# Row bounds as 16 rows of the query tile, gate logits inside the value projections, and one form for every VectorE key tile, in a fused attention and feed-forward kernel

## The chip, the cores and the metric

The kernel runs on one core of one Trainium2 chip. The metric is device time in microseconds (us) of one execution. A core has TensorE (matrix multiply, PE), VectorE (DVE), ScalarE (ACT), GpSimd (POOL) and SyncE (SP, which here issues nearly all DMAs). [...]

## The reference

```
x: (1, 2048, 512) bf16; 32 heads of 16; feed-forward width 1792
g = sigmoid((x * gate_w).sum(-1, keepdims=True))
q, k, v = split(x @ wqkv)                       # per head (2048, 16)
p = softmax(q @ k.T * 16 ** -0.5)
a = concat_heads(p @ v) @ wo
b = (silu(x @ w_gate) * (x @ w_up)) @ w_down
out = g * a + (1 - g) * b
```

## The kernel before

Queries are split into four blocks of 512 (`qb`), heads into eight groups of four (`g`). A unit is one block and one group, 32 units in all, and each has 16 key tiles of 128 keys: 512 key tiles. For one key tile the scores of four heads are four matrices of 128 keys by 512 queries; their exponentials are multiplied with the values by `pv`, four matmuls side by side (one per head) in the 32-column strips of the array, into one accumulating PSUM bank `o_ps`. Column 0 of each head's values is one, so row 0 of each strip sums the softmax denominators.

Two engines compute exponentials. ScalarE takes a key tile as two pairs of heads: `emit_pair` (line 741) writes scores to a two-bank tile `s_t` (two of them, in turn), one ACTIVATE of 128x1024 writes `e_t`. VectorE takes a whole key tile: `emit_d` (line 808) sends each head's scores to a one-bank tile `d_t`, and a scale, an addition and a conversion to uint16 make the bits of a rough bf16 exponential in `y` (tile names c_t, kaug, wd_t, by the buffer it was given). That is then refined in one of two ways, by `groups[n]`:

- 2: two mask instructions (`bits`, line 858) and one product (`product`, line 867) give two bf16 tiles, so two groups of four value matmuls;
- 4: three additions of constants (`copy`, line 850) give four tiles, so four groups of value matmuls.

`v_take` (line 1471) asks `quad` (line 1479): it gives 4 when the planned idle time of TensorE, summed in `spare`, is over `SPARE`, and else 2.

The softmax subtracts a bound instead of the row's maximum. A row of `kaug` (the keys, 32 rows per head) is constant, and the query tile's row 0 of each head holds minus the sum over 16 dimensions of |q| times the largest |k| of that dimension (`kb`, from `k_bound`, line 467). Rows 1 to 16 hold q and k. For the groups 1 to 7, `q_pieces` (line 532) projects the queries, copies them to `qst`, sends them by DMA to the query tiles `q1` and `qx` (`get_q`), and takes absolute values into `aq`; `bound_pieces` (line 600) multiplies `aq` with `kneg` on TensorE, copies the result to `bq` and sends it by DMA to row 0. Group 0 has its own path, which uses the same row.

The values of heads 4 to 31 are projected per key tile by `v_pieces` (line 507); `gate_pieces` (line 624) makes the gate's logits with 64 one-column matmuls, and `gate_end` (line 640) their exponential.

The order on each engine is not left to a scheduler. While the program is built, a planner keeps a time for each engine (`plan.pe`, `plan.dve`, `plan.act`), with a cost for each instruction (0.6 us for an eviction, `MUL_US` for a product), and emits instructions one by one; `ordered` ties each to the one before it on its engine. ScalarE's pairs come first. Gaps of TensorE are filled with value matmuls and with pieces of chains (projections, feed-forward, output), which `Pacer` picks by release and deadline in slots (one slot per key tile). `fill_dve` (line 887) gives VectorE the next thing that is ready. `v_unit` (line 1454) lets VectorE take another key tile from the end of a unit when it would be done in time; so the number of key tiles on VectorE, and with it that of ScalarE's exponentials, comes out of the planner. Everything but `s_t` and `o_ps` shares three PSUM banks (`m_tile`, line 358): `d_t`, projections, the feed-forward's `gu` and `dps`, the output's `ops`.

Of the kernel before, what the change touches and what calls it, by code (L numbers as in the profile page):

```python
# [79 lines left out]
def kernel(  # L80
# [46 lines left out]
    EXP_B = {4: 128.0 * (127.0 - math.log2(5.372947814979324)), 2: 128.0 * (127.0 - math.log2(1.5015118813815151))}  # L127
    MUL_US = 1.2
    TINY = 1e-37
    AHEAD = 1  # L130
    SPARE = 0.5

# [75 lines left out]
    def late_loads():  # L208
        queue.dma_start(out=gw_col[:], in_=gate_w.rearrange("(dc p) -> p dc", p=P))
        queue.dma_start(out=wo_t[:], in_=A_wo.rearrange("(b p) d -> p b d", p=P))  # L210
        for i in range(2):
            for j in range(4):
                h = H - 8 + 4 * i + j
                queue.dma_start(out=wo_l[32 * j + 1:32 * j + 1 + DH, i, :], in_=A_wo[h * DH:(h + 1) * DH, :])
# [41 lines left out]
    for g in (1, 2):  # L256
# [11 lines left out]

    pidx = const.tile([P, 1], F32, name="pidx")
    nc.gpsimd.iota(pidx[:], pattern=[[0, 1]], base=0, channel_multiplier=1,  # L270
                   allow_small_or_imprecise_dtypes=True)
    bsel = const.tile([P, 8], BF16, name="bsel")
    lo_t = const.tile([P, 8], F32, name="lo_t")
    for h in range(8):
        c = 2 * (h % 4) + h // 4
        nc.gpsimd.memset(lo_t[:, c:c + 1], float(DH * h))
    far_t = const.tile([P, 8], F32, name="far_t")
    nc.gpsimd.memset(wo_l[:], 0.0)
# [10 lines left out]
    kb = const.tile([P, NB], F32, name="kb")  # L289
    kneg = const.tile([P, NB, 8], BF16, name="kneg")  # L290
    gval = const.tile([P, KT], F32, name="gval")
# [156 lines left out]
    def k_pieces(b, tb):  # L448

        def end(t, p):  # L450
            vec.tensor_copy(out=kst[b][:, t * QBW:(t + 1) * QBW], in_=p[:, :])
            m_free(p, plan.dve)
            if t == QB - 1:
                for hh in range(8):
                    g, j = 2 * b + hh // 4, hh % 4
                    if g > 0:
                        queue.dma_start(out=kaug[32 * j + 1:32 * j + 1 + DH, g, :],
                                          in_=kst[b][DH * hh:DH * (hh + 1), :])

        def lhs(dc):  # L460
            if dc == 0 and tb == 0:
                kst[b] = (on_t[1], bblk)[b == 1][:, :, :].rearrange("p b q -> p (b q)")
            return wqk[:, dc, D + P * b:D + P * (b + 1)]
        return columns(DC, "kp", lhs, lambda dc: xT[:, dc, tb * QBW:(tb + 1) * QBW],
                       lambda p: later(0.6, lambda: end(tb, p)))

    def k_bound(b):
        vec.tensor_reduce(out=kb[:, b:b + 1], in_=kst[b][:, :], axis=AX.X, op=ALU.max, apply_absolute_value=True)
        vec.tensor_scalar(out=kneg[:, b, :], in0=bsel[:, :], scalar1=kb[:, b:b + 1],
                          scalar2=None, op0=ALU.mult)  # L470

# [35 lines left out]
    def v_pieces(tt):  # L507

        def end(p):
            dst = vaug[:, tt, 4 * VC:G * 4 * VC].rearrange("p (h c) -> p h c", c=VC)[:, :, 1:1 + DH]  # L510
            vec.tensor_copy(out=dst, in_=p[:, 64:D].rearrange("p (h c) -> p h c", c=DH))
            m_free(p, plan.dve)
        return columns(DC, "vp", lambda dc: xT[:, dc, tt * P:(tt + 1) * P], lambda dc: wv[:, dc, 64:D],
                       lambda p: later(0.54, lambda: end(p)), c0=64)

# [6 lines left out]
    for g in range(5, G):  # L522
# [3 lines left out]
          for qb in range(QB)]  # L526
    aqs = {}

# [3 lines left out]
    def q_pieces(qb, b):  # L532
        def landed(p):
            me = plan.chain
            later(0.6, lambda: end(p, me), key=("q", b))

        def end(p, me):
            qst = work.tile([P, QBW], BF16, tag="qst", name="qst")
            vec.tensor_copy(out=qst[:, :], in_=p[:, :])
            m_free(p, plan.dve)  # L540
            for hh in range(8):
                gg, j = hh // 4, hh % 4
                if (b, gg) != (0, 0):
                    queue.dma_start(out=get_q(qb, 2 * b + gg)[32 * j + 1:32 * j + 1 + DH, j % 2, :],
                                      in_=qst[DH * hh:DH * (hh + 1), :])

            def mag():
                aq = work.tile([P, QBW], BF16, tag="aq", name="aq", bufs=4)
                vec.tensor_scalar(out=aq[:, :].bitcast(U16), in0=qst[:, :].bitcast(U16),
                                  scalar1=0x7FFF, scalar2=None, op0=ALU.bitwise_and)  # L550
                aqs[(qb, b)] = aq
            plan.chain = me
            later(0.21, mag, plan.dve, ("q", b))
# [31 lines left out]
    def variants(p, to, q, more=()):  # L585
# [11 lines left out]
        for cost, f in more:  # L597
            later(cost, f, key=key)

    def bound_pieces(qb, b):  # L600

        st = {}

        def f():
            st["p"] = m_tile("bp")
            mm(st["p"][0:8, :], lhsT=kneg[:, b, :], rhs=aqs[(qb, b)][:, :], start=True, stop=True,
               tile_position=(0, 0))
            spend("C", 1)
            later(0.6, end)

        def end():
            bq = work.tile([8, QBW], BF16, tag="bq", name="bq")
            vec.tensor_copy(out=bq[:, :], in_=st["p"][0:8, :])
            m_free(st["p"], plan.dve)
            for j in range(4):
                if b == 0:
                    queue.dma_start(out=q1[32 * j:32 * j + 1, j % 2, :], in_=bq[2 * j + 1:2 * j + 2, :])
                else:
                    t = qx[(qb * (NB - 1) + b - 1) % 2]
                    queue.dma_start(out=t[32 * j:32 * j + 1, j % 2, :, :], in_=bq[2 * j:2 * j + 2, :])  # L620
        return [(1, f, True)]


    def gate_pieces(t0):
        def f():
            gp = m_tile("glog")
            for t in (t0, t0 + 1):
                for dc in range(DC):
                    mm(gp[:, t:t + 1], lhsT=xT[:, dc, t * P:(t + 1) * P],
                       rhs=gw_col[:, dc:dc + 1], start=(dc == 0), stop=(dc == DC - 1))  # L630
            spend("F", 2)

            def end():
                vec.tensor_scalar(out=ge[:, t0:t0 + 2], in0=gp[:, t0:t0 + 2], scalar1=-40.0, scalar2=40.0,
                                  op0=ALU.max, op1=ALU.min)
                m_free(gp, plan.dve)
            later(0.15, end)
        return [(0.7, f, True, "F", None)]

# [80 lines left out]
    groups = {}  # L720
    spare = [0.0]
    pv_turn = [True]
# [426 lines left out]
    for g in (3, 4):  # L1149
        ones_rows(vec, g)  # L1150

    vec.tensor_scalar(out=lo_t[:], in0=lo_t[:], scalar1=pidx[:, 0:1], scalar2=None, op0=ALU.subtract)
    vec.tensor_scalar(out=far_t[:], in0=lo_t[:], scalar1=-float(DH) + 0.5, scalar2=-1.0,
                            op0=ALU.is_gt, op1=ALU.mult)
    vec.scalar_tensor_tensor(out=bsel[:, :], in0=lo_t[:], scalar=0.5, in1=far_t[:],
                                   op0=ALU.is_lt, op1=ALU.mult)
    plan.act = plan.pe
# [54 lines left out]
    q_of[0] = again  # L1212
    v_rest = [pace.add(v_pieces(tt), 2, int(12 + 3 * tt)) for tt in range(KT)]

# [14 lines left out]
    for qb in range(QB):  # L1229
        for b in range(NB):  # L1230
# [16 lines left out]
            else:  # L1247
                rel = UNIT.index((qb, 2 * b - 2)) * KT + 1 if (qb, b) != (0, 2) else UNIT.index((0, 2)) * KT + 1
            q = pace.add(q_pieces(qb, b), rel, d - 25)
            bc = pace.add(bound_pieces(qb, b), rel, d - 22, [q] + after, 2)  # L1250
            need.setdefault(d - 12, []).append(bc)
            for g in {max(2 * b, 1), 2 * b + 1}:
                q_of[UNIT.index((qb, g))] = bc
    gates = [pace.add(gate_pieces(2 * i), 36 + 7 * i, 44 + 7 * i) for i in range(KT // 2)]
    gates = [pace.add([(0.2, gate_end, False)], 40, 106, gates)]
    turned = pace.add([(1, turn_odds, True, "F", None)], 40, 130, gates, 2)
# [120 lines left out]
    def begin(n):  # L1377
        plan.slot = n
        for c in need.get(n, []):
            force(c)  # L1380
        if n == 28:
            late_loads()
# [88 lines left out]
    def v_take():  # L1471
        un = v_unit()
        hi[un] -= 1
        n = un * KT + hi[un]
        groups[n] = 2 if quad() else 4
        forward()
        return n

    def quad():
        if spare[0] > SPARE:  # L1480
            spare[0] = 0.0
            return False
        return True

# [10 lines left out]
    while au < UNITS:  # L1495
# [10 lines left out]
        if room > 0.02:  # L1506
# [17 lines left out]
            if room > 0.4 and closed in o_of and 0 < pvs[closed] and pv_left(closed) > 1 and (closed or pvs[0] != KT // 2) and sum(  # L1524
# [5 lines left out]
                spend("C", 1)  # L1530
                spare[0] += 0.22
                continue
            if room > 0.15:
                plan.pe += 0.1
                spare[0] += 0.1
                continue
# [98 lines left out]
```

## Time and profile before

| | |
|---|---|
| three runs, median (range) | 780.24 us (780.03 to 782.4) |
| the profiled execution | 780.74 us; span in the profile 778.8 us |
| granted TensorE clock | 0.999 |
| busy of the span: ScalarE, TensorE, VectorE | 764.5, 740.7, 725.5 us |
| first and last exponential of ScalarE start at | 13.16 us, 769.7 us |
| DMA | 32.63 MB in 88138 packets |

A line of the costliest groups reads: source line, engine, operation, output<-input by tile names, partitions x elements and type, count | busy us, mean ns of one | idle time just before them and what ended it. All instructions that the planner orders carry the line of the helper (163, 166, 175), so tile names tell them apart. Instructions of one engine overlap a little: the time from start to start is shorter than one's duration. A wait is read as: who waited <- for whom: total us, times, the longest.

### The profile page before, as it was taken

The page shows a single profiled execution, that of the slowest core. Times are in us where ns is not written, and L with a number is a line of the kernel's source. Part 1 is how long each engine was busy: PE and PEld are TensorE (multiplying, and loading weights), DVE is VectorE, ACT ScalarE, POOL GpSimd, SP SyncE. Part 2 cuts the span into 40 slices and gives each one's busy share as a digit, 9 for nine tenths or more (in the row PEclk, how much of TensorE's full clock was granted, in tenths as well). Part 3 has the DMA queues.
Part 4 walks back from the last instruction along what each step waited for, and adds up shares of the span by engine and source line. Part 5 has one row for each costly group of instructions (what it writes and reads, how often), then busy time and mean ns, then how long its engine had stood idle before and what let it go on. Part 6 is the DMA issues. An engine that isn't in the chain of part 4 may idle for free.

```text
span 778.8 us, 21608 instructions
## 1 busy us (share of the span) xinstructions
PE 740.7 (95%) x8877; PEld 223.6 (29%) x8877; DVE 725.5 (93%) x1162; ACT 764.5 (98%) x863; POOL 11.0 (1%) x34
## 2 busy tenths in 40 slices
PE   8999999999999999999999999989999989999997
PEld 3322333322222222232222222222222322222222
DVE  7799999899889999999999999999999999999994
ACT  5999999999999999999999999999999999999996
POOL 5000000000000000000000000000000000000000
PEclk9999999999999999999999999999999999999999
DMA  8002103134110112220100131211001222100001
GB/s 189 2 5 49 29 20 79 50 99 94 43 32 8 27 37 62 51 53 20 32 15 19 31 94 26 66 28 34 13 20 27 60 66 45 46 12 12 15 29 35
DMA packets 88138, 32.63 MB, mean 42 GB/s; under 512 B 74304, under 2 KB 87592, under 8 KB 88040
## 3 DMA queue, kind: packets, MB, share of 16 engines
q1 hardware_dynamic: 86312, 30.93, 16.5%
q8 instruction: 69, 1.13, 0.6%
q10 hardware_dynamic: 1728, 0.33, 0.2%
q14 instruction: 29, 0.24, 0.1%
HBM read 21.55 MB, written 2.35 MB: 31 GB/s over the span
## 4 chain that ended last, share of the span: by engine, by line
ACT 56%; PE 24%; issue 12%; DVE 7%; ACTq 0%; DVEq 0%
ACT e_t L166 53%; PE s_t L163 9%; PE o_ps L163 6%; PE gu L163 5%; DVE c_t L175 4%; ACT th L166 3%; PE qp L163 1%; PE dps L163 1%; DVE mt L175 1%; PE warm L163 1%; PE vp L163 1%; PE kp L163 1%; DVE gs L175 0%; PE ops L163 0%; DVE kaug L175 0%
## 5 line engine op out<-in xcount | busy, mean ns | idle before, releaser
L166 ACT ACTIVATE e_t<-s_t 128x1024 bf16<-128x1024 f32 x794 | 743.7, 1147 | 0.9 <-PE s_t L163 0.8
L175 DVE TENSOR_SCALAR c_t<-d_t 128x512 uint16<-128x512 f32 x404 | 267.8, 683 | 17.7 <-PE d_t L163 17.0
L163 PE MATMUL s_t<-qx,kaug 32*128 32x512 bf16 (+1 forms) x1252 | 244.3, 382 | 21.7 <-ACT e_t L166 19.6
L163 PEld LDWEIGHTS <-kaug 32*128 32x128 bf16 (+1 forms) x2048 | 97.9, 91 | 339.4 <-issue 334.6
L163 PE MATMUL o_ps<-e_t,vaug 128*32 128x512 bf16 x1588 | 154.9, 386 | 0.0
L175 DVE TENSOR_SCALAR c_t<-c_t 128x2048 uint16<-128x2048 uint16 x193 | 129.9, 685 | 1.1
L163 PE MATMUL d_t<-qx,kaug 32*128 32x512 bf16 x380 | 128.5, 384 | 0.0
L163 PE MATMUL o_ps<-c_t,vaug 128*32 128x512 bf16 x1028 | 97.8, 385 | 0.6 <-DVE osb L175 0.6
L163 PEld LDWEIGHTS <-vaug 128*32 128x32 bf16 x2800 | 59.5, 94 | 100.3 <-issue 94.2
L163 PE MATMUL gu<-xT,wg 128*32 128x512 bf16 x896 | 73.0, 384 | 0.0
L175 DVE TENSOR_TENSOR c_t<-c_t 128x2048 bf16<-128x2048 bf16 x59 | 71.7, 1215 | 0.0
L163 PE MATMUL gu<-xT,wu 128*32 128x512 bf16 x896 | 68.3, 382 | 0.1
L163 PE MATMUL ops<-wd_t,mt 128*32 128x512 bf16 x672 | 57.1, 382 | 0.0
L163 PE MATMUL s_t<-q,kaug 32*128 32x512 bf16 (+1 forms) x204 | 39.8, 382 | 6.0 <-ACT e_t L166 5.1
L175 DVE SCALAR_TENSOR_TENSOR gs<-th,gu 128x512 bf16<-128x512 bf16 x56 | 38.2, 682 | 3.4 <-ACT th L166 3.0
L175 DVE SCALAR_TENSOR_TENSOR mt<-gs,gu 128x512 bf16<-128x512 bf16 x56 | 38.2, 682 | 3.2 <-PE gu L163 1.5
L166 ACT ACTIVATE th<-gu 128x512 bf16<-128x512 f32 x56 | 40.9, 731 | 0.0
L175 DVE TENSOR_SCALAR kaug<-d_t 128x512 uint16<-128x512 f32 x52 | 34.8, 682 | 1.5 <-PE d_t L163 1.2
L163 PEld LDWEIGHTS <-mt 128*32 128x32 bf16 (+1 forms) x1037 | 24.1, 95 | 27.5 <-issue 21.6
L163 PEld LDWEIGHTS <-wu 128*32 128x32 bf16 x896 | 19.5, 95 | 24.1 <-issue 15.2
L163 PEld LDWEIGHTS <-wg 128*32 128x32 bf16 x896 | 17.4, 94 | 24.3 <-issue 21.8
L175 DVE TENSOR_SCALAR kaug<-c_t 128x2048 uint16<-128x2048 uint16 x35 | 24.0, 686 | 0.3
(149 smaller groups left out, 449.0 us busy)
## 6 DMA issues: line engine op xcount, KB each, us to landing
wg<-in_B_w_gate_dram SPq DMA_DIRECT2D x56, 128.0 KB
wu<-in_B_w_up_dram SPq DMA_DIRECT2D x56, 128.0 KB
on<-osb SPq DMA_DIRECT2D x120, 16.0 KB
rb<-rr SPq DMA_DIRECT2D x15, 128.0 KB
wd_t<-in_B_w_down_dram SPq DMA_DIRECT2D x7, 256.0 KB
qx<-qst SPq DMA_DIRECT2D x96, 16.0 KB
out_dram<-o_t SPq DMA_DIRECT2D x12, 128.0 KB
kaug<-on SPq DMA_DIRECT2D x20, 64.0 KB
```

The source lines that it names most:

```text
L163: return ordered(nc.tensor.matmul(*args, **kw))
L166: ordered(nc.scalar.activation(*args, **kw))
L175: return lambda *a, **kw: ordered(f(*a, **kw))
```

## The change

For groups 1 to 7, q and k now lie in rows 0 to 15 of a head's 32, and rows 16 to 31 hold the bound's 16 terms unsummed: the queries' signs are set to minus, and the result is multiplied by `kb` (a second VectorE instruction), and goes by eight (or four) more DMAs of 16 rows to the query tile. The keys' rows there are the constant that already filled the tile. The bound's matmul, its eviction and its DMAs of single rows go; a query projection now waits for the keys' maxima. The gate's weights are loaded at slot 3 instead of 28 and copied into column 63 of the value weights, which the first value projection has used by then; each of the 16 projections computes columns 63 to 511 and clips its first column into `ge`. The functions `bound_pieces`, `gate_pieces` and `quad` go whole, with what makes `kneg` and its selection matrix. Every VectorE key tile takes masks and product, and the planner's cost of a product goes from 1.2 to 1.135.

```diff
-    MUL_US = 1.2
+    MUL_US = 1.135
-    SPARE = 0.5
+    QLEAD = 24
...
     def late_loads():
-        queue.dma_start(out=gw_col[:], in_=gate_w.rearrange("(dc p) -> p dc", p=P))
...
-    bsel = const.tile([P, 8], BF16, name="bsel")
-    lo_t = const.tile([P, 8], F32, name="lo_t")
...
-    kneg = const.tile([P, NB, 8], BF16, name="kneg")
...
                     if g > 0:
-                        queue.dma_start(out=kaug[32 * j + 1:32 * j + 1 + DH, g, :],
-                                          in_=kst[b][DH * hh:DH * (hh + 1), :])
+                        queue.dma_start(out=kaug[32 * j:32 * j + DH, g, :], in_=kst[b][DH * hh:DH * (hh + 1), :])
...
     def k_bound(b):
         vec.tensor_reduce(out=kb[:, b:b + 1], in_=kst[b][:, :], axis=AX.X, op=ALU.max, apply_absolute_value=True)
-        vec.tensor_scalar(out=kneg[:, b, :], in0=bsel[:, :], scalar1=kb[:, b:b + 1],
-                          scalar2=None, op0=ALU.mult)
...
     def v_pieces(tt):
...
+            vec.tensor_scalar(out=ge[:, tt:tt + 1], in0=p[:, 63:64], scalar1=-40.0, scalar2=40.0, op0=ALU.max, op1=ALU.min)
             vec.tensor_copy(out=dst, in_=p[:, 64:D].rearrange("p (h c) -> p h c", c=DH))
             m_free(p, plan.dve)
-        return columns(DC, "vp", lambda dc: xT[:, dc, tt * P:(tt + 1) * P], lambda dc: wv[:, dc, 64:D],
-                       lambda p: later(0.54, lambda: end(p)), c0=64)
+        return columns(DC, "vp", lambda dc: xT[:, dc, tt * P:(tt + 1) * P], lambda dc: wv[:, dc, 63:D],
+                       lambda p: later(0.69, lambda: end(p)), c0=63)
...
     def q_pieces(qb, b):
...
+        def rows(t, r):
+            for hh in range(8):
+                gg, j = hh // 4, hh % 4
+                if (b, gg) != (0, 0):
+                    queue.dma_start(out=get_q(qb, 2 * b + gg)[32 * j + r:32 * j + r + DH, j % 2, :],
+                                      in_=t[DH * hh:DH * (hh + 1), :])
...
-            for hh in range(8):
-                gg, j = hh // 4, hh % 4
-                if (b, gg) != (0, 0):
-                    queue.dma_start(out=get_q(qb, 2 * b + gg)[32 * j + 1:32 * j + 1 + DH, j % 2, :],
-                                      in_=qst[DH * hh:DH * (hh + 1), :])
+            rows(qst, 0)
+
+            aq = work.tile([P, QBW], BF16, tag="aq", name="aq")

             def mag():
-                aq = work.tile([P, QBW], BF16, tag="aq", name="aq", bufs=4)
-                vec.tensor_scalar(out=aq[:, :].bitcast(U16), in0=qst[:, :].bitcast(U16),
-                                  scalar1=0x7FFF, scalar2=None, op0=ALU.bitwise_and)
-                aqs[(qb, b)] = aq
+                vec.tensor_scalar(out=aq[:, :].bitcast(U16), in0=qst[:, :].bitcast(U16), scalar1=0x8000, scalar2=None,
+                                  op0=ALU.bitwise_or)
+                plan.chain = me
+                later(0.21, weigh, plan.dve, ("q", b))
+
+            def weigh():
+                vec.tensor_scalar(out=aq[:, :], in0=aq[:, :], scalar1=kb[:, b:b + 1], scalar2=None, op0=ALU.mult)
+                rows(aq, DH)
...
-    def bound_pieces(qb, b):
...
-    def gate_pieces(t0):
...
-    v_rest = [pace.add(v_pieces(tt), 2, int(12 + 3 * tt)) for tt in range(KT)]
+
+    def gate_column():
+        later(0.1, lambda: vec.tensor_copy(out=wv[:, :, 63:64], in_=gw_col[:].unsqueeze(2)))
+    gate_w_in = pace.add([(0.2, gate_column, False)], 9, 11, [v_late])
+    v_rest = [pace.add(v_pieces(tt), 2, int(14 + 3 * tt), [gate_w_in]) for tt in range(KT)]
...
-            q = pace.add(q_pieces(qb, b), rel, d - 25)
-            bc = pace.add(bound_pieces(qb, b), rel, d - 22, [q] + after, 2)
-            need.setdefault(d - 12, []).append(bc)
+            q = pace.add(q_pieces(qb, b), rel, d - QLEAD, after)
+            need.setdefault(d - 12, []).append(q)
...
-    gates = [pace.add(gate_pieces(2 * i), 36 + 7 * i, 44 + 7 * i) for i in range(KT // 2)]
-    gates = [pace.add([(0.2, gate_end, False)], 40, 106, gates)]
+    gates = [pace.add([(0.2, gate_end, False)], 40, 106, v_rest)]
...
+        if n == 3:
+            queue.dma_start(out=gw_col[:], in_=gate_w.rearrange("(dc p) -> p dc", p=P))
...
-        groups[n] = 2 if quad() else 4
+        groups[n] = 2
...
-    def quad():
-        if spare[0] > SPARE:
-            spare[0] = 0.0
-            return False
-        return True
...
-                spare[0] += 0.22
...
-                spare[0] += 0.1
```

## The prediction

> **What bounds the kernel now.** I read the page first, then the stages of 40 us, then who waits for whom, then the timeline. The page's busy shares and its costliest groups (count, then busy us and mean ns of one):
>
> ```profile
> PE 740.7 (95%) x8877; PEld 223.6 (29%) x8877; DVE 725.5 (93%) x1162; ACT 764.5 (98%) x863; POOL 11.0 (1%) x34
> L166 ACT ACTIVATE e_t<-s_t 128x1024 bf16<-128x1024 f32 x794 | 743.7, 1147 | 0.9 <-PE s_t L163 0.8
> L175 DVE TENSOR_SCALAR c_t<-d_t 128x512 uint16<-128x512 f32 x404 | 267.8, 683 | 17.7 <-PE d_t L163 17.0
> L175 DVE TENSOR_SCALAR c_t<-c_t 128x2048 uint16<-128x2048 uint16 x193 | 129.9, 685 | 1.1
> L175 DVE TENSOR_TENSOR c_t<-c_t 128x2048 bf16<-128x2048 bf16 x59 | 71.7, 1215 | 0.0
> ```
>
> ScalarE's 794 exponentials (two per key tile, so 397 of 512 key tiles) fill it; in front of all of them it stood idle for 0.9 us. The other 115 key tiles go through VectorE. The end moves with the number of exponentials as long as ScalarE is fed, and the question is whether it stays fed. The stages (length, then busy us of PE, PEld, DVE, ACT) show how it does beside a full VectorE:
>
> ```profile
> 60.00:100.00 40.00, 38.98 (x473) 12.11 (x465) 39.74 (x63) 40.00 (x45) 0.00 (x0) 1.00 0.17 35
> 140.00:180.00 40.00, 39.22 (x493) 11.71 (x489) 35.86 (x61) 40.00 (x47) 0.00 (x0) 1.00 0.28 71
> 300.00:340.00 40.00, 37.57 (x460) 11.19 (x452) 39.52 (x65) 40.00 (x48) 0.00 (x0) 1.00 0.20 47
> 420.00:460.00 40.00, 38.53 (x469) 11.38 (x461) 39.53 (x61) 39.97 (x47) 0.00 (x0) 1.00 0.17 43
> ```
>
> VectorE is idle between 0.3 and 4.1 us of 40, and ScalarE is full in all four. The waits of TensorE (total us, times, longest) say how near a late VectorE is to being felt:
>
> ```profile
> PE s_t L163 <- ACT e_t L166: 25.3, 77, 1.0
> PE s_t L163 <- DVE mt L175: 1.2, 2, 0.9
> PE o_ps L163 <- DVE osb L175: 0.6, 2, 0.4
> ```
>
> TensorE waits 25 us for ScalarE to free score banks. It never waits for an eviction of the three shared PSUM banks (d_t, gu, ops, qp). Last, what an instruction really occupies (start, us):
>
> ```profile
> 399.63 13.06 ACT L166 ACTIVATE e_t<-s_t 128x1024 bf16<-128x1024 f32 x14
> 409.21 0.67 DVE L175 TENSOR_SCALAR c_t<-c_t 128x2048 uint16<-128x2048 uint16 x1
> 409.81 0.67 DVE L175 TENSOR_SCALAR c_t<-d_t 128x512 uint16<-128x512 f32 x1
> 410.41 1.20 DVE L175 TENSOR_TENSOR c_t<-c_t 128x2048 bf16<-128x2048 bf16 x1
> 411.54 1.27 DVE L175 TENSOR_SCALAR c_t<-d_t 128x512 uint16<-128x512 f32 x2
> ```
>
> Starts lie closer than durations: 0.60 us for an eviction or a mask, 1.13 us for a product. Fourteen exponentials give (13.06 - 1.147)/13 = 0.916 us from one to the next.
>
> **ScalarE: the term that sets the end.** The list of the changed program's instructions holds 790 exponentials instead of 794, and 117 VectorE key tiles (468 evictions) instead of 115 (460). Four exponentials at 0.916 us are 3.7 us (at the group's 743.7/794 = 0.937, 3.75 us). Everything else on ScalarE is unchanged, and so are the first exponentials and the order behind the last one (ten score and value groups, the reciprocal, the last four projections).
>
> **VectorE.** All 117 tiles now take two masks and one product; before, 79 did and 36 took three shifted copies. Counts from the two programs, prices from the rows above and these:
>
> ```profile
> L175 DVE CAST bq<-bp 8x512 bf16<-8x512 f32 x16 | 10.8, 673 | 0.8 <-PE bp L163 0.6
> L175 DVE TENSOR_SCALAR aq<-qst 128x512 uint16<-128x512 uint16 x16 | 4.6, 285 | 0.0
> L175 DVE TENSOR_SCALAR on<-qst,vsel 128x512 bf16<-128x512 bf16 x4 | 1.2, 346 | 0.0
> ```
>
> - masks and copies 266 to 234: -32 x 0.60 = -19.2
> - products 79 to 117: +38 x 1.13 = +42.9
> - evictions of d_t: +8 x 0.60 = +4.8
> - bq copies gone: -16 x 0.60 = -9.6
> - the new product of aq with kb, 16 times: the trace lacks it. Below it lies aq<-qst at 0.20 us from start to start, above it on<-qst,vsel at 0.35 us in full; the second has the same types and a per-partition scalar too, and with the overlap of the others (0.08) it is 0.27, so +4.3 (3.2 to 5.6)
> - gate clips, 8 of 0.15 to 16: +1.2; kneg (four of 0.23), three small preparations and one new gate-column copy: about -1.2
>
> Sum +23 us. Before, VectorE stood idle for 36 us of the 720 us from 20 to 740; that leaves some 13.
>
> By stretches of 45 exponentials, in each program's own order and at these prices, VectorE's work was 603 us against ScalarE's 637 between exponentials 90 and 765, and over ScalarE's in two of fifteen stretches, by 1% at most. Now it is 635 us against 637, and over it in eight, by 1.6 to 2.9% in five of them. ScalarE adds about 0.016 us per exponential in waits for TensorE (0.916 against the 0.90 seen between undisturbed starts), 11 us there. So VectorE has 13 us left, and needs 0.3 to 0.5 us per 40 in its fullest stages, 4 to 8 us here. It fits, barely. I take the cost on the path at nothing; the cover is this 13 us, and its loss is the first rival.
>
> **TensorE and its banks.** 272 matmuls with copies are gone, 68 groups of four at about 0.22 us (eight take 0.61, four 0.39): -15 us. 16 bound matmuls at 0.22: -3.5; 64 gate matmuls: -2.7; two groups of e_t less, four groups of filler more: +0.4. 24 uses of a shared bank go, eight come. Value matmuls get a 449th column that starts one bf16 element earlier; nothing in the trace starts so, between 357 ns as now and twice that for 64 groups is 0 to 10 us, all before 110 us. I take 0, since the element count is what the vp rows follow (357 ns for 448, 383 for 512). All this is off the path while ScalarE is full.
>
> **SP queue.** 64 bound-row DMAs become 112, +48 at about 0.58 us of issue, 28 us spread over sixteen places. Behind them stand weight loads, osb rows and outputs. From the last row's issue to its first reader there are 19 to 40 exponentials (17 us or more), 16 to 33 before, where no wait showed. The gate weights' transfer goes from 59.9 us to behind the first loads at about 13 us; the column copy stands at exponential 20 (32 us). Cost 0; if rows came late, ScalarE would stop for the whole delay.
>
> **Sum.** The profiled execution took 780.74 us, 1.9 more than its span, and is 0.5 over the median. 780.74 - 3.7 = 777.0; against the median 780.24 - 3.7 = 776.5. About 0.3%, 2.3 us, is what a measurement of this kernel can tell from no change.
>
> **Rivals.**
> 1. VectorE becomes the bound in its dense stretches (slower). Place: exponentials 135 to 180, 270 to 315, 405 to 450, 540 to 585, 675 to 720. Starts that come later than an instruction's own 0.60 or 1.13 us by up to 0.2 us make 15 us of 740 in the trace, 2%. Where VectorE's work with these 2% exceeds ScalarE's time with its waits, the excess is 0.9 to 1.5 us in each of these five (smaller in four others), and if no stretch gives anything back it adds to 7 us: 776.5 + 7.2 = 783.7. It decides once VectorE is later than a bank is spare, after which TensorE stops at d_t, the next scores are late and ScalarE idles. For: only 13 us of cover. Against: the three full stages above with ScalarE at 40.00, and no TensorE wait on an eviction.
> [...]
> 2. Half of that excess stays and the rest is given back by neighbouring stretches: 776.5 + 3.5 = 780.0, no change. For: sums over pairs of stretches give 3 to 5 us instead of 7.
> 3. TensorE's relief of 21 us takes away waits of ScalarE too. It has about 0.016 x 790 = 13 us of them, most behind a group that TensorE began just before; a third less is -4: 772.5. Against: the order still fills each gap to the brim with feed-forward work.
> 4. Fewer exponentials not being there is excluded by the program's list; what may fail is a late aq row or gate column, one stop of some us, which I put into rivals 1 and 2.
>
> **Chances.** Forecast (up to 777.9) 0.43, rival 3 0.12, rival 2 (777.9 to 782.6) 0.19, rival 1 0.26. Faster is 0.55, same 0.19, slower 0.26. The range leaves out a little of rival 3 below and the worse half of rival 1 above: 772.5 to 784.5.
>
> **What would show it.** Right: 790 exponentials without idle time in front of them, VectorE at 95 to 97%, its wait for d_t well below 17 us, and TensorE still waiting for ScalarE alone. Wrong: TensorE waiting for VectorE at d_t or gu, ScalarE below 40.00 in the dense stages, c_t products after which o_ps waits, an aq product far from 0.27 us, or s_t waiting for a DMA of aq.

## The result, and the profile after

The changed kernel takes 784.83 us (median of 20 runs, 781.54 to 787.09) against 780.81 us before (20 runs, 780.03 to 782.51): ratio 1.005, 95% interval 1.004 to 1.0059. It is slower by 4 us, where 4 us faster was forecast. The profiled execution took 785.19 us, its span is 783.2 us.

The page's busy shares and the costliest groups after (count, busy us and mean ns of one, idle time in front and what ended it):

```profile
PE 724.5 (93%) x8533; PEld 219.1 (28%) x8533; DVE 741.2 (95%) x1178; ACT 761.8 (97%) x859; POOL 10.6 (1%) x25
L166 ACT ACTIVATE e_t<-s_t 128x1024 bf16<-128x1024 f32 x790 | 739.2, 1135 | 8.2 <-PE s_t L163 4.2
L175 DVE TENSOR_SCALAR c_t<-d_t 128x512 uint16<-128x512 f32 x404 | 266.9, 685 | 7.8 <-PE d_t L163 7.1
L163 PE MATMUL gu<-xT,wg 128*32 128x512 bf16 x896 | 72.2, 390 | 5.6 <-DMA wg<-in_B_w_gate_dram 3.8
```

The four exponentials are gone, but ScalarE now stands idle for 8.2 us in front of the others, where it was 0.9. From the first exponential's start to the last one's it takes 761.0 us instead of 756.5. Counting all that comes on top of the undisturbed 0.903 us between starts (0.477 behind a tanh), ScalarE's waits rise from 13.1 to 21.2 us: +8.1 against -3.6 for the exponentials, which is the 4.5. The stages tell where (length, then busy us of PE, PEld, DVE, ACT, POOL, then the granted clock):

```profile
100.00:140.00 40.00, 36.78 (x423) 10.32 (x421) 36.59 (x56) 38.12 (x43) 0.00 (x0) 0.96 0.29 62
140.00:180.00 40.00, 36.71 (x436) 11.52 (x428) 39.75 (x66) 40.00 (x48) 0.00 (x0) 1.00 0.24 65
340.00:380.00 40.00, 35.72 (x422) 10.31 (x418) 36.29 (x57) 37.27 (x44) 0.00 (x0) 0.96 0.18 42
420.00:460.00 40.00, 37.90 (x465) 10.93 (x457) 39.82 (x62) 40.00 (x46) 0.00 (x0) 1.00 0.14 35
460.00:500.00 40.00, 35.07 (x402) 10.84 (x404) 37.30 (x60) 38.24 (x45) 0.00 (x0) 0.96 0.26 64
```

ScalarE loses time in three stages, and in these VectorE is less busy than in the full ones beside them. The waits (total us, times, longest) name what is late. PEld is TensorE's loading of its weights, and wg holds the `w_gate` weights of one chunk of the feed-forward:

```profile
PE s_t L163 <- ACT e_t L166: 40.2, 115, 1.0
PEld L163 <- DMA wg<-in_B_w_gate_dram: 6.3, 3, 2.5
PE gu L163 <- DMA wg<-in_B_w_gate_dram: 3.8, 2, 2.2
PE gu L163 <- DVE c_t L175: 1.6, 1, 1.6
ACT e_t L166 <- PE s_t L163: 4.2, 5, 2.4
ACT e_t L166 <- PE d_t L163: 3.5, 4, 1.4
```

Before, no line had wg in it. TensorE stops three times at the first matmul of a feed-forward chunk, because the chunk's `w_gate` weights have not arrived; the scores behind it in TensorE's order are late, and ScalarE idles. One of the three stands under VectorE's c_t, since a product there ends 0.01 us before the matmul starts. It is the weights all the same: the PEld line counts all three, and in e1 below, where the weights are early, that matmul starts 0.5 us before the product does. In the timeline of SP, which issues the loads in order, and of TensorE:

```profile
356.07 0.54 SPq L175 DMA_DIRECT2D dd<-osb  x1
356.66 2.42 SPq L175 DMA_DIRECT2D on<-osb  x4
359.19 5.42 SPq L175 DMA_DIRECT2D qx<-qst  x8
364.70 4.96 SPq L175 DMA_DIRECT2D qx<-aq  x8
369.70 0.58 SPq L175 DMA_DIRECT2D wg<-in_B_w_gate_dram  x1
```
```profile
370.99 0.39 PE L163 MATMUL d_t<-qx,kaug 32*128 32x512 bf16 x1
373.59 0.76 PE L163 MATMUL gu<-xT,wg 128*32 128x512 bf16 x8 [2.21 <-DMA wg<-in_B_w_gate_dram]
374.82 1.04 PE L163 MATMUL gu<-xT,wg 128*32 128x512 bf16 x8
```

SP issues DMAs without a pause from 356 to 370 us, the weights last. TensorE is ready for them at 371.4 and starts 3.9 us after their issue. The kernel before sends four short DMAs of the bound (qx<-bq) where now there are eight (qx<-aq). In front of the first feed-forward chunk its queue is otherwise the same, and shows how much that load had to spare:

```profile
105.94 4.93 SPq L175 DMA_DIRECT2D qx<-qst  x8
112.03 2.55 SPq L175 DMA_DIRECT2D qx<-bq  x4
114.62 0.40 SPq L175 DMA_DIRECT2D wg<-in_B_w_gate_dram  x1
```
```profile
120.52 0.83 PE L163 MATMUL gu<-xT,wg 128*32 128x512 bf16 x12
```

That is 5.9 us from issue to use, the least of the 56 `w_gate` loads of that profile. After, the load is issued at 111.29 us and TensorE is ready for it at 112.4: 4.8 us less. The queue took 1.9 us of them (from the first row's issue to the weights' it is 10.6 us instead of 8.7), and the changed order of TensorE's work 2.9 us (from the first row's issue to the need it is 11.7 us instead of 14.6).

At the other two stops the order of SP's queue changed as well. The load for the chunk at 371 us was issued in front of the rows before, 23 us ahead of its use:

```profile
348.51 0.37 SPq L175 DMA_DIRECT2D wg<-in_B_w_gate_dram  x1
361.05 4.94 SPq L175 DMA_DIRECT2D qx<-qst  x8
366.09 2.50 SPq L175 DMA_DIRECT2D qx<-bq  x4
```
```profile
371.57 0.39 PE L163 MATMUL gu<-xT,wg 128*32 128x512 bf16 x4
```

The load for the third stop's chunk was issued 8.9 us ahead (482.90 to 491.79 us). After, both stand behind the eight new DMAs. These take 2.4 to 3.1 us longer than the four of before at the three places, and the stops are 1.6 to 2.2 us. So with the old DMAs in the new order the loads would be just in time; this is an estimate that leaves out waits for what the DMAs read, and no run has that order with the old DMAs.

### The profile page after: what moved, and what is told of

Same layout as the page of the kernel before. It is cut to its first block, busy times and chain, and to the rows that moved or that the text cites. A ratio compares the mean times of both kernels' runs of the same rounds, so it can differ in the third digit from the quotient of the medians.

```text
span 783.2 us, 20976 instructions
## 1 busy us (share of the span) xinstructions
PE 724.5 (93%) x8533; PEld 219.1 (28%) x8533; DVE 741.2 (95%) x1178; ACT 761.8 (97%) x859; POOL 10.6 (1%) x25
## 4 chain that ended last, share of the span: by engine, by line
ACT 51%; PE 20%; DVE 14%; issue 13%; DMA 1%; SPq 1%; ACTq 0%; DVEq 0%
ACT e_t L166 47%; DVE c_t L175 9%; PE s_t L163 7%; PE o_ps L163 4%; ACT th L166 3%; PE gu L163 3%; PE ops L163 2%; DVE kaug L175 1%; DVE mt L175 1%; PE kp L163 1%; DVE gs L175 1%; PE qp L163 1%; DMA wg<-in_B_w_gate_dram 1%; PE warm L163 1%; SPq L175 1%
## 5 line engine op out<-in xcount | busy, mean ns | idle before, releaser
L163 PE MATMUL d_t<-qx,kaug 32*128 32x512 bf16 x384 | 131.4, 385 | 0.0
L175 DVE TENSOR_SCALAR c_t<-c_t 128x2048 uint16<-128x2048 uint16 x166 | 111.7, 686 | 0.3
L175 DVE TENSOR_TENSOR c_t<-c_t 128x2048 bf16<-128x2048 bf16 x87 | 106.0, 1218 | 0.0
L163 PEld LDWEIGHTS <-vaug 128*32 128x32 bf16 (+1 forms) x2536 | 55.6, 94 | 96.0 <-issue 90.1
L163 PE MATMUL o_ps<-c_t,vaug 128*32 128x512 bf16 x792 | 76.9, 388 | 1.2 <-DVE osb L175 1.1
L163 PE MATMUL s_t<-q,kaug 32*128 32x512 bf16 (+1 forms) x192 | 37.6, 385 | 7.6 <-ACT e_t L166 7.0
L175 DVE TENSOR_SCALAR kaug<-d_t 128x512 uint16<-128x512 f32 x60 | 40.2, 685 | 4.0 <-PE d_t L163 4.0
L175 DVE TENSOR_SCALAR osb<-o_ps,tiny 128x512 bf16<-128x512 f32 x30 | 22.4, 745 | 1.0 <-PE o_ps L163 1.0
```

Source lines behind the costliest of these rows:

```text
L163: return ordered(nc.tensor.matmul(*args, **kw))
L175: return lambda *a, **kw: ordered(f(*a, **kw))
```

## The experiments

Theory A: the weight loads are late because SP issues them behind more DMAs of bound rows. Theory B, the forecast's first rival: VectorE has become the bound. Each time measured is a median, and the ratio beside it is to the kernel before on the same chip.

**e1: weights early.** The first three chunks are loaded at slot 28, and the others three chunks ahead instead of two.

```diff
-    ffnw = ctx.enter_context(tc.tile_pool(name="ffnw", bufs=3))
+    ffnw = ctx.enter_context(tc.tile_pool(name="ffnw", bufs=4))
...
-                if i == 0:
-                    w_load(0, True)
...
-                w_load(i + 2, True)
-                w_load(i + 2, False)
+                w_load(i + 3, True)
+                w_load(i + 3, False)
...
         if n == 28:
+            for i in range(3):
+                w_load(i, True)
+                w_load(i, False)
             late_loads()
```

> The changed kernel, but the feed-forward weights of the first three chunks are loaded at slot 28, and each later chunk is loaded three chunks ahead instead of two, into four buffers instead of three. The planner's order on TensorE, VectorE and ScalarE is the same (790 exponentials); only SP's order differs. Theory A (late weight loads behind the bound-row DMAs): the three TensorE stops at about 112, 371 and 494 us go, ScalarE's waits fall from 21 us to the 13 us of before, and the time is four exponentials below the kernel before: 776 to 778 us. Theory B (VectorE has become the bound, the weights are a symptom): VectorE's work is unchanged, so the time stays at 783 to 786 us and the stops come back at d_t or gu as waits for VectorE.

Measured: 777.7 us, ratio 0.9965 (0.9953 to 0.9978). ScalarE's waits are 12.7 us. In its waits no line with wg is left, and the three stages are full:

```profile
100.00:140.00 40.00, 37.95 (x455) 11.39 (x453) 38.88 (x60) 40.00 (x47) 0.00 (x0) 1.00 0.24 50
340.00:380.00 40.00, 37.68 (x455) 11.46 (x453) 39.34 (x62) 40.00 (x47) 0.00 (x0) 1.00 0.17 39
460.00:500.00 40.00, 36.01 (x431) 11.60 (x427) 39.87 (x65) 40.00 (x48) 0.00 (x0) 1.00 0.26 59
```

VectorE does the same work in the same order and is fuller than in the changed kernel (39.87 of 40), and ScalarE is at 40.00. This is theory A's outcome.

**e3: eight more DMAs ahead of the bound rows.**

```diff
             rows(qst, 0)
+            for hh in range(8):
+                queue.dma_start(out=junk[DH * hh:DH * (hh + 1), :], in_=qst[DH * hh:DH * (hh + 1), :])
```

> The changed kernel with eight more DMAs of 16 rows (from qst to a tile that nobody reads) in front of each bound's rows: the suspected delay of SP's queue doubled, with nothing else changed on any engine. Theory A: each of the places where weights stand behind the bound rows is late by another 4.6 us, so three stops of 2 to 3 us become stops of 6 to 8, and places that were just covered show too: 797 to 815 us. Theory B: 783 to 786 us, since no engine has more work.

Measured: 812.0 us, ratio 1.0401 (1.0387 to 1.0415). The queue and the wait:

```profile
101.57 5.84 SPq L175 DMA_DIRECT2D qx<-qst  x8
107.46 5.01 SPq L175 DMA_DIRECT2D junk<-qst  x8
112.57 5.36 SPq L175 DMA_DIRECT2D qx<-aq  x8
117.98 0.58 SPq L175 DMA_DIRECT2D wg<-in_B_w_gate_dram  x1
```
```profile
120.69 0.62 PE L163 MATMUL gu<-xT,wg 128*32 128x512 bf16 x4 [7.43 <-DMA wg<-in_B_w_gate_dram]
```
```profile
PE gu L163 <- DMA wg<-in_B_w_gate_dram: 25.6, 6, 7.4
```

Where there were three stops there are now five of 2.1 to 7.4 us, and one of 0.2. From issue to use the weights take 2.7 us here, and 2.6 at this place in the changed kernel: it is their place in the queue that is late, not the transfer that is slower. No engine had more work, so theory B has no place for the 27 us on top of the changed kernel.

**e4: the row bounds alone, on the kernel before.**

> The kernel before with the row bounds alone changed to 16 rows (gate logits, copies by TensorE's idle time and the product's cost of 1.2 as before). The planner keeps 794 exponentials. Theory A: SP's queue has the same eight bound-row DMAs in front of the first weights, so at least one TensorE stop of 2 to 3 us waiting for wg, and 782 to 787 us. Theory B: VectorE has about 5 us less work than before (16 evictions of 0.60 against 16 products of 0.27), so it is no slower than the kernel before: 779 to 781 us.

Measured: 787.02 us, ratio 1.0085 (1.0072 to 1.0099), with VectorE 4.6 us less busy than before (720.9 us). Its worst stop is elsewhere, at the same kind of place (the other two are 1.1 and 0.6 us):

```profile
312.29 5.79 SPq L176 DMA_DIRECT2D qx<-qst  x8
318.18 4.96 SPq L176 DMA_DIRECT2D qx<-aq  x8
323.24 0.53 SPq L176 DMA_DIRECT2D wg<-in_B_w_gate_dram  x1
```
```profile
326.43 0.45 PE L164 MATMUL gu<-xT,wg 128*32 128x512 bf16 x4 [2.76 <-DMA wg<-in_B_w_gate_dram]
```

**e6: the row bounds alone, weights early** (the edit of e1 on e4).

> The row bounds alone, as in e4_rows_alone, with the weights of the feed-forward loaded early (slot 28, three chunks ahead, four buffers). 794 exponentials. Theory A: the 6.6 us that e4_rows_alone cost go, 779 to 781 us, ScalarE's waits back at 13 us. If part of e4's loss came from the rows themselves (late rows, a wait for aq), that part stays, 782 us or more.

Measured: 781.28 us, ratio 1.001 (1.0001 to 1.0019), and no TensorE wait for `w_gate`. It is 1.0 us above the kernel before, and a little above the 779 to 781 us expected, so 5.6 us of e4's 6.6 were the weights. ScalarE's waits are 13.9 us. What is left is no late row: ScalarE stops for 0.7 us at 104 us, in e4 too, where TensorE waits 0.5 us for VectorE's copy of a value projection.

**e5: masks and product alone, on the kernel before** (`groups[n] = 2`, `MUL_US = 1.135`).

> The kernel before with the third part of the change alone: every VectorE key tile by masks and product, cost of a product 1.135. The planner keeps 794 exponentials, and no DMA is added. Theory A (what costs is SP's queue in front of the weights): the time of the kernel before, 780 to 782 us, no wait of TensorE for wg. Theory B (VectorE's load costs): VectorE gets some 19 us more work at the same number of exponentials, so 784 us or more.

Measured: 782.01 us, ratio 1.0015 (1.0004 to 1.0026). The profiled execution (780.51 us) has VectorE busy for 740.1 us and ScalarE's waits at 13.3 us, against theory B. The runs lie between 780.51 and 784.81: the five with a granted clock of 0.999 or 1.0 take 780.51 to 780.90 us, the six with 0.992 to 0.998 take 782.01 us or more. The profiled one is of the first kind, so what lowers the clock in the others is open.

**e9 and e10: which loads.** e9 loads only the first two chunks early (two ahead afterwards, three buffers); e10 loads three ahead, but the first ones where they were.

> The changed kernel with the first two chunks of weights loaded at slot 28, but later chunks still two ahead in three buffers. Theory A puts one stop (at 112 us, 2.6 us of ScalarE's waits) down to the first loads and two (at 371 and 494 us, 3 us each) down to loads two chunks ahead: the first goes, the others stay, 781 to 784 us.

> The changed kernel with weights three chunks ahead in four buffers, but the first loads where they were, behind the bound rows. Theory A: the stop at 112 us stays (or grows by the one load more that is issued there, 0.5 us each for gate and up), the other two go: 779 to 782 us.

Measured: e9 782.49 us (ratio 1.0027, 1.0016 to 1.0039), e10 779.8 us (0.999, 0.9981 to 0.9999). e9's profile keeps TensorE's stops at 369.4 and 491.9 us and has none near 112; e10's keeps the one at 112.3 us and has no other. Each against its own kernel before, e1 is at -2.7 us, e10 at -0.8, e9 at +1.9 and the changed kernel at +4.0: the first stop costs 1.9 us, the other two 4.6, together 6.5 of the 6.7 between e1 and the changed kernel.

**e11: control.** The kernel before with its first two chunks early.

> Control: the kernel before with the first two chunks of weights loaded at slot 28. It has no TensorE wait for weights, so theory A expects nothing: 780 to 781 us. If early weights are worth something in themselves, below 779 us, and then e1_weights_early says less about the change.

Measured: 780.56 us, ratio 1.0004 (0.9995 to 1.0012). Early weights are worth nothing where they were not late.

**e7 and e8: how much room VectorE has.** On e1, 59 or 117 additions that nobody reads, unknown to the planner.

```diff
         vec.tensor_tensor(out=c.bitcast(BF16), in0=y.bitcast(BF16), in1=c.bitcast(BF16), op=ALU.mult)
+        vec.tensor_scalar(out=junk[:, :], in0=still[:, :], scalar1=1.0, scalar2=None, op0=ALU.add)
```

> e1_weights_early with 59 more VectorE instructions (uint16 128x384 additions on a tile that nobody reads, behind every second product), which the planner does not know of: about 0.17 us each from start to start, 10 us of work. It measures how much room VectorE has left. By the estimate of 13 us of cover the time stays within 1 us of e1_weights_early: 777 to 779 us. If VectorE is already the bound, it rises by about the 10 us added: 786 to 788 us.

> As e7_vector_extra_59 with 117 such instructions, 20 us of work. By the estimate of 13 us of cover 7 us of it show: 783 to 787 us. If VectorE is the bound already, about 20 us: 796 to 798 us. If late VectorE work is only felt through a bank now and then, less than 3 us: below 781 us.

Measured: e7 779.2 us (ratio 0.9983, 0.9974 to 0.9993), e8 787.71 us (1.0087, 1.0073 to 1.0101). An addition lasts 0.253 us in both traces; less the 0.08 us by which VectorE's masks overlap (0.68 us long, 0.60 apart) that is 0.17 us from start to start, an estimate that agrees with the expected one. Over e1 the first 10 us of work cost 1.5 us and 20 us cost 10.0, both a little more than the 13 us of cover gave: about 10 us are free, and what comes after is paid nearly in full. In e8, TensorE waits for VectorE (none of the o_ps lines was over 0.8 us in e1):

```profile
PE o_ps L163 <- DVE osb L175: 4.6, 8, 1.2
PE o_ps L163 <- DVE c_t L175: 2.0, 7, 0.4
PE gu L163 <- DVE mt L175: 1.3, 3, 0.7
```

**e2: weights early, and the choice of three copies back.** The edit of e1, and `quad` with what feeds it as before the change. The planner arrives at 786 exponentials.

> As e1_weights_early, and the choice between product and three copies by TensorE's planned idle time is back. The planner then gives 786 exponentials. Theory A: each exponential less is 0.916 us, so 7.3 us below the kernel before, 772 to 775 us. Theory B: copies take 0.53 us of VectorE less than a product's tile, so this one gains much more over e1_weights_early than the four exponentials (3.7 us): 8 us or more.

Measured: 773.14 us, ratio 0.9904 (0.9891 to 0.9918), 7.2 us below the kernel before and 4.6 below e1, of which the four exponentials explain 3.7. It beats both kernels. So with early weights the third part of the change (masks and product for every tile) costs 4.6 us, and in e5 it alone took no exponential away. Copies spend idle TensorE time to spare VectorE 0.53 us a tile (two masks and a product are 2 x 0.60 + 1.13 us from start to start, three copies 3 x 0.60), and with that the planner gives VectorE two more key tiles.

## Why the prediction was wrong

- **Four exponentials less, 3.7 us**: right. The count is 790, and e1, where they stay fed, is 2.7 us below the kernel before by medians, 1 us less than forecast. In the profiles, from the first exponential's start to the last one's, e1 is 4.0 us shorter; in front of the first and behind the last its profiled run is longer than that of before.
- **VectorE fits, barely, with 13 us left**: right. In e1 VectorE is idle for 15.7 us of the 720 (36.2 before), the room is about 10 us (e7, e8), and its wait for d_t fell from 17.0 to 7.1 us in the changed kernel. The new product's row is 348 ns, against the 346 taken from on<-qst,vsel. The first rival had the right sign, and its 783.7 us comes near the 784.83 by luck, for a reason that e1 rules out; its point of decision lies some 10 us of VectorE work further on.

```profile
L175 DVE TENSOR_SCALAR aq<-aq,kb 128x512 bf16<-128x512 bf16 x16 | 5.6, 348 | 0.0
L163 PE MATMUL vp<-rb,xT 128*32 128x449 bf16 x256 | 19.1, 359 | 0.0
```

- **The 449th value column, 0 of 0 to 10 us**: right, 359 ns against 357. The upper bound was too low: a group takes 0.20 us from start to start in the changed kernel, so 64 groups at twice that would be some 13 us more, not 10. The factor of two was the author's guess; no run shows it.
- **SP queue, cost 0**: this step failed. It counted 48 DMAs at 0.58 us, named the weight loads behind them, and then worked out the lead of only one thing, the rows themselves (whose waits are indeed at most 0.2 us). The weights were taken as covered without a reason. In place of 0, ScalarE's waits grew by 8.1 us, more than the 3.6 us that four exponentials gave. For the first chunk the lead was to be had from the profile of before: 5.9 us, of which a load takes 2.6 to 3.9 us from issue to use where TensorE waits for it. The 2 to 3 us left go to the longer queue (1.9 us) and the changed order (2.9 us). For the other two stops the profile of before shows leads of 23 and 8.9 us and would have warned of nothing; there the changed order put the loads behind the rows. Spreading 28 us over sixteen places hid that only the worst places count.
- **Rival 4 was too narrow**: a late transfer as "one stop of some us" was there, but tied to aq rows and the gate column, and without a price or a place of its own.
- **TensorE's relief (rival 3)**: not seen. ScalarE's waits in e1 are 12.7 us against 13.1; TensorE only waits more for ScalarE (41.2 us instead of 25.3), and e2 is what that idle time is worth.

## What to carry to other kernels

When an edit adds DMAs to an in-order queue, list what stands behind them and work out, for each, the time from issue to first use in the profile of before, less its transfer time; the smallest remainder decides, not the average. Do it in the order of the changed program: an edit that moves work can put a load behind the new DMAs that stood in front of the old ones. VectorE, 98% busy in e1 from 20 to 740 us beside the ScalarE that sets the end, took some 10 us more of work (1.3% of the span) for 1.5 us of time: add dummy work to such an engine to learn how much room it has. Earlier loads, at the price of one more buffer, were worth 6.7 us here (e1 against the changed kernel, each beside its own kernel before).

## What the runs showed of the hardware

TensorE stood still for 1.6, 2.2 and 1.6 us in the three stops, and behind each the granted clock was 0.50 for 3.41 us; the eight gu matmuls at 374.82 take 1.04 us, eight at 369.31, in front of the stop, 0.61. In the changed kernel's trace the six changes of the clock from 114 to 500 us lie 3.41, 256.00, 3.41, 119.47 and 3.41 us apart, which is 1, 75, 1, 35 and 1 times 3.413. Cut at these places, the stretches of the second and third stop of the changed kernel and the one behind each:

```profile
370.53:373.94 3.41, 1.20 (x23) 0.25 (x15) 2.76 (x4) 2.07 (x3) 0.00 (x0) 1.00 0.50 111
373.94:377.35 3.41, 3.41 (x32) 0.53 (x24) 0.87 (x2) 2.36 (x3) 0.00 (x0) 0.50 0.55 124
493.40:496.81 3.41, 1.78 (x29) 0.43 (x21) 2.12 (x4) 1.97 (x3) 0.00 (x0) 1.00 0.74 168
496.81:500.22 3.41, 3.41 (x32) 0.82 (x28) 2.13 (x4) 3.10 (x4) 0.00 (x0) 0.50 0.30 68
```

The same for the second stop of e9, of 1.32 us:

```profile
490.97:494.38 3.41, 2.08 (x33) 0.54 (x25) 2.42 (x4) 2.27 (x4) 0.00 (x0) 1.00 0.73 165
494.38:497.79 3.41, 3.29 (x46) 1.04 (x38) 3.13 (x6) 3.41 (x5) 0.00 (x0) 1.00 0.32 70
```

With TensorE busy for 1.20 or 1.78 of 3.41 us (1.81 at the first stop) the next stretch has half the clock, with 2.08 the full one. Cut in the same way from 20 us on and without the last 12 us, the changed kernel's trace has 219 stretches. The three at full clock in which TensorE was idle longest, for 65, 48 and 47%, were followed by half clock; the others, with 33% or less, were not. Its gaps of 1.01 us (in front of 526.19) and 0.94 us (295.33) left the clock at 1.00. So a stop of 1.6 us was enough here and one of 1.32 us (e9) was not; where between them the clock changes, and why, no run shows.

Of ScalarE's 8.1 us, 5.2 are its idle time just behind the three stops (1.3, 2.4 and 1.4 us), and 1.9 more fall in or just behind the stretches at half clock. The 20 runs point the same way: the one with a granted clock of 0.999 took 781.54 us, the ten with 0.995 took 784.6 us (median), the seven with 0.993 785.2 us. So some 3 us of the changed kernel's time is the slow clock; this is an estimate that rests on one run without it.
